# A fused attention and expert kernel: two PSUM banks become one tile, and copies at two seams are regrouped

## The chip, the cores and the metric

The kernel runs on one core of one Trainium2 chip. The metric is the device time of one execution in microseconds (us); the time given for a kernel is the median of several executions. A profiled execution shows a span, from its first to its last instruction, and a granted clock of TensorE.

## The reference

The first half is causal attention over blocks of 64 rows: 8 batches of 8 heads, 576 rows of 64 values each. The second half sends every one of the 4608 rows to one of 8 experts.

```python
scores = scale * np.matmul(q, k.transpose(0, 1, 3, 2))   # B=8 H=8 S=576 D=64
mask = block_i >= block_j                                 # blocks of 64 rows
...
attn_out = np.matmul(softmax(scores), v)
x = attn_out.transpose(0, 2, 1, 3).reshape(B * S, H * D)  # 4608 x 512
logits = x @ w_gate                                       # 8 experts
expert_idx = np.argmax(logits, axis=1)
gate_w = probs[np.arange(N), expert_idx]
...
h = np.maximum(x_sorted[lo:hi] @ w1[e], 0.0)              # 512 -> 1024
y_sorted[lo:hi] = h @ w2[e]                               # 1024 -> 512
return gate_w[:, None] * y
```

## The kernel before

**Attention** goes by pairs of heads, 32 of them. A loop over p holds the steps of one pair and of its neighbours, and the order in which the loop is written is the order of each engine's queue (the schedule is manual; only the semaphore waits are put in by the framework, which finds them from which tiles instructions read and write). In step p TensorE (PE) computes scores(p+1), which ScalarE (ACT) turns into exponentials; then attend(p), ten or so products with V, first into `o0` (128 columns of the PSUM bank `mix`) and then into `oP` (another bank); then trans(p+2), nine transposes of the next Q and K into the bank `sA`, which `copies` moves to SBUF; then turn_back(p-1), logits(p-1) and denominators(p). GpSimd (POOL) casts Q and K of pair p+2 to 16 bits in `h16`, of which there is one buffer. `keep(p)` copies `o0` and `oP` to SBUF on ACT in two instructions (L307 and L308). `s4` is two strips of 64 score columns, one at the end of `mix` and one at the end of `oP`, with one exponential each.

Once per batch, in six pairs of the loop and again near its end, the step also holds shares() (an exponential on ACT, L391), ranks() (matmuls into columns 192 to 239 of `mix`, L402 and L406) and count(). They choose the experts of the batch before. These pairs are called ranked pairs below; in a ranked pair ranks() stands in PE's queue right behind trans(p+2).

**The opening** does pairs 0 and 1 ahead of the loop. The transposes of pair 1 go to `oP` (eight) and `mix` (one), and VectorE (DVE) copies the two parts to SBUF. Then POOL makes the constants of attention and of routing, and `wg`, and only then comes the loop, whose first step holds the cast of pair 2 (L222 on POOL).

**The hand-over** is the last step of the loop and what follows. Rows sorted by expert are worked on in pages of 128: m1 (L634) multiplies with w1, m2 (L645) with w2. The stationary operand of m1 is first copied out of the weight store `wall` by mstage (128x4096 in 16 bits), for page 0 on ACT (L626) and for page 1 and all later ones on DVE (L627). mexpert loads the page's expert number into a register. Page 0's m1 is cut in two halves around the last turn_back and logits; settle (L338) reads the strip that logits and denominators write in the bank `sB`, and m1(1) writes over that bank.

Of the kernel before, what the change touches and what calls it, by code (L numbers as in the profile page):

```python
# [15 lines left out]
ds = bass.ds  # L16
# [6 lines left out]
def kernel(  # L23
# [40 lines left out]
    sC = psum.tile([128, 2, 512], F32, name="sC")  # L64
    oP = psum.tile([128, 512], F32, name="oP")
    mix = psum.tile([128, 512], F32, name="mix")
    sA16, sB16, sC16 = (t.rearrange("p h f -> p (h f)").bitcast(F16) for t in (sA, sB, sC))
    back = sC.rearrange("p h f -> p (h f)")
    o0, s4, strip = mix[:, 0:128], (mix[:, 128:192], oP[:, 448:512]), sB[:, 0, 0:160]

# [191 lines left out]
    def scores(p):  # L262

        pt, acc, p4, qkT = pts[p % 2], accs[p % 2], p4s[p % 2], qkTs[p % 2]
        a, b, c = ((t[:, 0], t[:, 1]) for t in (sA, sB, sC))
        low = slice(0, 64)
        for h in range(2):
            r = slice(h * 64, h * 64 + 64)
            nc.tensor.matmul(out=s4[h], lhsT=qkT[r, 1, 448:576], rhs=qkT[r, 0, 512:576],
                             start=True, stop=True, skip_group_check=True)  # L270
        for h in range(2):
            exp(p4[:, h], s4[h])
        score(p, 0, a, 0, 128, 448)
        score(p, 0, a, 448, 0, 64)
        exp(pt[:, :, 0:448], sA[:, :, 0:448])
        exp(acc[low, :, 0:64], sA[low, :, 448:512])
        score(p, 2, c, 256, 320, 256)
        score(p, 0, c, 0, 64, 64)
        score(p, 1, c, 64, 128, 64)
        score(p, 3, c, 128, 384, 64)  # L280
        score(p, 2, c, 192, 256, 64)
        exp(pt[:, :, 1152:1408], sC[:, :, 256:512])
        exp(low_blocks(pt[low]), sC[low, :, 64:192].rearrange("p h (c x) -> p h c x", c=2))
        exp(pt[low, :, 1088:1152], sC[low, :, 192:256])
        exp(acc[:, :, 64:128], sC[:, :, 0:64])
        score(p, 1, b, 0, 192, 384)
        score(p, 3, b, 384, 448, 128)
        exp(pt[:, :, 512:896], sB[:, :, 0:384])
        exp(pt[:, :, 960:1088], sB[:, :, 384:512])
# [14 lines left out]

    def keep(p):
        oT = oTs[p % 2]
        nc.scalar.activation(oT[:, 0:128], o0, AF.Copy)  # L307
        nc.scalar.activation(oT[:, 128:576], oP[:, 0:448], AF.Copy)  # L308

# [274 lines left out]
    tags = [t[:, 256:258] for t in xss]  # L584
    stages = [t.rearrange("p h f -> p (h f)").bitcast(F16)[:, 0:4096] for t in pts]
    hTs = [t.rearrange("p n f -> p (n f)")[:, 0:1024] for t in qkTs]
    ys = [t.rearrange("p c h d -> p (c h d)")[:, 0:512] for t in vts[0:3]] + \
# [35 lines left out]

    def mstage(T, engine=nc.vector):
        src = wall[:, ds(pg["e", T], 1), 0:8, :].rearrange("p a n f -> p (a n f)")
        did = nc.scalar.activation(stages[T % 2], src, AF.Copy) if engine is nc.scalar \  # L626
            else engine.tensor_copy(stages[T % 2], src)  # L627
        read_of(did, T)

    def m1(T, part=range(8)):  # L630
        hp = hps[T % 2]
        for f in part:
            for c in range(4):
                nc.tensor.matmul(  # L634
                    out=hp[:, f // 4, f % 4 * 128:f % 4 * 128 + 128],
                    lhsT=stages[T % 2][:, c * 1024 + f * 128:c * 1024 + f * 128 + 128],
                    rhs=xTs[T % XS][:, c, :], start=(c == 0), stop=(c == 3),
                    skip_group_check=True)
# [42 lines left out]
    with tc.manual_schedule(engines={ET.PE, ET.Activation, ET.DVE, ET.Pool, ET.SP}):  # L681
# [11 lines left out]
        trans(0, ((sC16, 0, 5), (sB16, 5, 9)), (nc.scalar, nc.vector))()  # L693
        cast(1, (nc.vector, 0, 5), (nc.gpsimd, 5, 9))
        scores(0)
        trans(1, ((oP.bitcast(F16), 0, 8), (mix.bitcast(F16), 8, 9)), (nc.vector, nc.vector))()
        for _ in range(12):
            nc.tensor.transpose(sA16[:, 0:128], ident16, ident16)
        constants()
        routing_constants()  # L700
        for h in range(2):
            r = slice(h * 64, h * 64 + 64)
            nc.sync.dma_start(
                out=gate[r], in_=moe_w_gate.rearrange("(p h d) e -> h d p e", h=2, d=64)[h])
            nc.gpsimd.tensor_copy(wg[r, :, h * E:h * E + E], gate[r, :, ::-1])
        slots_of = [p for p in range(3, PAIRS - 5) if p % HP < 3]
# [10 lines left out]
        for p in range(PAIRS + 1):  # L717
# [17 lines left out]
            if p + 2 < PAIRS:  # L735
                cast(p + 2)
            for b, j in scatters.get(p, ()):
                scatter(b, j)
# [9 lines left out]
            if left == 1:  # L748
                mexpert(0, ET.Activation)
                mstage(0, nc.scalar)  # L750
            if nxt:
# [3 lines left out]
            if now:  # L755
                attend(p)
                keep(p)
                sums(p)
            if p == PAIRS:
                m1(0, range(0, 4))  # L760
            if left == 3:
                weigh()
            turned = trans(p + 2) if p + 2 < PAIRS else None
            if done >= 0 and ranked:
# [29 lines left out]
            if left == 3:  # L794
                first_rows()
            if left == 1:
                mexpert(1)
                mstage(1)
        rest = rest_pages()
# [58 lines left out]
```

## Time and profile before

| What | Value |
|---|---|
| time, median of 3 | 354.7 us (354.23 to 354.81) |
| the profiled execution | 354.11 us |
| its span, and what lies around it | 352.2 us, 1.9 us |
| granted clock, mean | 0.993 |
| PE busy | 331.8 us, 94% of the span |
| ACT busy | 239.0 us, 68% |
| DVE busy | 225.1 us, 64% |
| POOL busy | 172.6 us, 49% |

The shares are means over three parts that have different limits: the opening (to about 20 us), the pairs (20 to 200 us) and the pages (from about 208 us). In the rows further down a row of the timeline gives the start of a group of like instructions, its length, the engine, the line, what is written and read, the count, and in brackets the idle time of the engine just before it with what ended it. Ends of matmuls are modelled.

### The profile page before, as it was taken

What the parts mean: (1) busy time and instruction counts of PE and PEld (TensorE: products, weight loads), DVE (VectorE), ACT (ScalarE), POOL (GpSimd) and SP (SyncE); (2) the same over time, 40 slices, a digit from 0 to 9 for tenths busy, and PEclk for the clock granted to TensorE, in tenths of its full rate; (3) what the DMA queues carried; (4) which work ended last, traced back from release to release, by engine and by line L of the source; (5) the groups of instructions that cost most, each with busy time, mean ns of one, the idle gap of its engine ahead of it and who ended that gap; (6) DMA issues with size and microseconds to landing.
All of it is one profiled execution on the core that took longest, in us unless ns stands there. A gap on an engine that the chain in (4) does not pass through costs nothing. (4 is left out here: it accounts for less than half of the span.)

```text
span 352.2 us, 11512 instructions
## 1 busy us (share of the span) xinstructions
PE 331.8 (94%) x4232; PEld 226.0 (64%) x4232; DVE 225.1 (64%) x516; ACT 239.0 (68%) x533; POOL 172.6 (49%) x216
## 2 busy tenths in 40 slices
PE   5899999999999999999999989899999999999980
PEld 4566666676666576656666567567677777777750
DVE  3557688788787887887889988683343434433330
ACT  3889898989898989989888824343454545544540
POOL 2821426647547557475586058768434342233231
PEclk9999999999999999999999999999999999999997
DMA  8999999999999999999999959999999899343531
GB/s 174 216 216 215 211 218 224 251 247 260 255 241 232 248 231 242 238 253 246 240 194 215 133 84 171 181 210 155 182 199 178 162 144 182 77 138 96 111 87 52
DMA packets 96803, 67.04 MB, mean 190 GB/s; under 512 B 71776, under 2 KB 80992, under 8 KB 96736
## 3 DMA queue, kind: packets, MB, share of 16 engines
q1 hardware_dynamic: 78816, 34.62, 52.5%
q0 software_dynamic: 17632, 30.98, 44.3%
q8 instruction: 37, 0.61, 0.8%
q10 hardware_dynamic: 288, 0.59, 0.7%
q14 instruction: 30, 0.25, 0.3%
HBM read 61.93 MB, written 15.77 MB: 221 GB/s over the span
## 5 line engine op out<-in xcount | busy, mean ns | idle before, releaser
L627 DVE COPY pt<-wall 128x4096 f16 x39 | 50.0, 1283 | 69.8 <-PE sB L634 33.4
L634 PEld LDWEIGHTS <-pt 128*128 128x128 f16 x1216 | 70.8, 98 | 12.2 <-issue 2.5
L300 PE MATMUL oP<-pt,v 128*64 128x448 f32 (+2 forms) x320 | 50.8, 459 | 0.0
L645 PEld LDWEIGHTS <-qkT 128*128 128x128 f16 x304 | 28.2, 98 | 28.3 <-ACT qkT L640 1.0
L640 ACT ACTIVATE qkT<-sA 128x1024 f16<-128x1024 f32 x19 | 19.4, 1023 | 36.5 <-PE sA L634 28.1
L427 POOL DMA_INDIRECT xsorted<-x,slot x30 | 37.3, 1243 | 11.4 <-POOL slot L426 7.9
L222 POOL CAST h<-qk 128x1152 f16<-128x1152 f32 (+2 forms) x20 | 22.3, 1114 | 38.8 <-PE sA L235 19.1
L634 PE MATMUL sB<-qk,pt 128*128 128x128 f16 x608 | 37.6, 219 | 2.4 <-DVE lr L338 1.3
L640 ACT ACTIVATE qkT<-sB 128x1024 f16<-128x1024 f32 x19 | 19.4, 1022 | 29.0 <-PE sB L634 29.0
L300 PEld LDWEIGHTS oP<-pt,v 128*64 128x64 f32 x320 | 22.5, 137 | 23.4 <-issue 18.4
L221 ACT ACTIVATE qkT<-sA 128x576 f16<-128x576 f16 x60 | 35.8, 650 | 2.3 <-PE sA L235 0.9
L634 PE MATMUL sA<-qk,pt 128*128 128x128 f16 x608 | 37.2, 219 | 0.0
L645 PE MATMUL sC<-wall,qkT 128*128 x152 | 35.9, 379 | 0.6 <-ACT qkT L640 0.6
L645 PE MATMUL oP<-wall,qkT 128*128 x152 | 35.9, 379 | 0.3 <-issue 0.2
L260 ACT ACTIVATE pt<-sB 128x768 f32<-128x768 f32 x64 | 35.0, 614 | 0.0
L654 POOL DMA_INDIRECT out_dram<-v,to x18 | 19.7, 1094 | 27.9 <-ACT v L650 26.0
L260 ACT ACTIVATE pt<-sC 128x512 f32<-128x512 f32 (+2 forms) x96 | 32.6, 414 | 0.9 <-PE mix L300 0.7
L300 PE MATMUL oP<-pt,wall 128*64 128x448 f32 (+2 forms) x192 | 30.4, 459 | 0.0
L260 ACT ACTIVATE pt<-sA 128x896 f32<-128x896 f32 x32 | 29.4, 918 | 0.2
L358 DVE TENSOR_TENSOR x<-sC,rec 128x640 f16<-128x640 f32 x24 | 19.8, 824 | 15.2 <-PE sC L352 14.5
L222 POOL CAST h<-wall 128x1152 f16<-128x1152 f32 x12 | 13.7, 1142 | 26.3 <-PE sA L235 16.8
L426 POOL TENSOR_SCALAR slot<-sl 128x1 int32<-128x1 f32 x40 | 14.4, 359 | 19.7 <-DVE sm L395 19.5
(185 smaller groups left out, 608.9 us busy)
## 6 DMA issues: line engine op xcount, KB each, us to landing
wall<-in_moe_w_dram POOLq DMA_DIRECT2D x32, 512.0 KB
qk<-in_q_dram SPq DMA_DIRECT2D x20, 288.0 KB
v<-in_v_dram SPq DMA_DIRECT2D x44, 128.0 KB
qk<-in_k_dram SPq DMA_DIRECT2D x18, 288.0 KB
wall<-in_v_dram SPq DMA_DIRECT2D x28, 128.0 KB
wall<-in_q_dram SPq DMA_DIRECT2D x12, 288.0 KB
wall<-in_k_dram SPq DMA_DIRECT2D x12, 288.0 KB
xsorted<-v SPq DMA_DIRECT2D x2, 516.0 KB
```

What stands on the lines that cost most here:

```text
L221: return nc.scalar.activation(dst, src, AF.Copy)
L222: return engine.tensor_copy(dst, src)
L260: nc.scalar.activation(dst, src, AF.Exp, scale=scale)
L300: nc.tensor.matmul(out=o[h * 64:h * 64 + 64], lhsT=vt[:, c, h, :] if c < 4 else v4[:, 2 * (p % HP) + h, :], rhs=src[:, h], start=(c == 0), ...
L358: nc.vector.tensor_tensor(out=x16[:, :, hp * 128:hp * 128 + 128].rearrange("p i (h d) -> p i h d", h=2), in0=back[:, 0:640].rearrange("p ( ...
L426: nc.gpsimd.tensor_single_scalar(slot, small[f"sl{b % 2}"][:, j:j + 1], 128.0, op=ALU.add)
L427: did = nc.gpsimd.indirect_dma_start(out=xsorted[:, :], out_offset=bass.IndirectOffsetOnAxis(ap=slot[0:m, :], axis=0), in_=x16s[b % 3][0:m ...
L627: else engine.tensor_copy(stages[T % 2], src)
L634: nc.tensor.matmul(out=hp[:, f // 4, f % 4 * 128:f % 4 * 128 + 128], lhsT=stages[T % 2][:, c * 1024 + f * 128:c * 1024 + f * 128 + 128], r ...
L640: nc.scalar.activation(hTs[T % 2], hp.rearrange("p a f -> p (a f)"), AF.Relu)
L645: did = nc.tensor.matmul(out=yp, lhsT=hT[:, f * 128:f * 128 + 128], rhs=wall[:, ds(pg["e", T], 1), 8 + f, :].rearrange("p a f -> p (a f)") ...
L654: did = nc.gpsimd.indirect_dma_start(out=out[:, :], out_offset=bass.IndirectOffsetOnAxis(ap=to, axis=0), in_=y, in_offset=None, bounds_che ...
```

## The change

Four edits.

1. The banks `mix` and `oP` become the two halves of one tile `out2`, and the two strips of `s4` are read by one exponential. `keep` is split into keep_first and keep_rest, with the same two copies.
2. In the opening the transposes of pair 1 lie in one piece in `out2`, and DVE copies them in two instructions of 576 columns (K, then Q). The cast of pair 1 is divided seven to two between DVE and POOL, it was five to four. The routing constants and `wg` stand behind the cast of pair 2 (the third cast).
3. In the step p = 0 the copies of trans(2) go to two engines, K to DVE and Q to ACT. Both had been on ACT.
4. At the hand-over ACT copies the w1 of page 0 in two halves, the second between keep_first and keep_rest, and then that of page 1 in three pieces into three buffers that are free by then; DVE no longer copies page 1.

```diff
-    oP = psum.tile([128, 512], F32, name="oP")
-    mix = psum.tile([128, 512], F32, name="mix")
-    sA16, sB16, sC16 = (t.rearrange("p h f -> p (h f)").bitcast(F16) for t in (sA, sB, sC))
+    out2 = psum.tile([128, 2, 512], F32, name="out2")
+    mix, oP = out2[:, 0], out2[:, 1]
+    sA16, sB16, sC16, out16 = (t.rearrange("p h f -> p (h f)").bitcast(F16)
+                               for t in (sA, sB, sC, out2))
     back = sC.rearrange("p h f -> p (h f)")
-    o0, s4, strip = mix[:, 0:128], (mix[:, 128:192], oP[:, 448:512]), sB[:, 0, 0:160]
+    o0, s4, strip = mix[:, 0:128], out2[:, :, 448:512], sB[:, 0, 0:160]
...
-        for h in range(2):
-            exp(p4[:, h], s4[h])
+        exp(p4, s4)
...
-    def keep(p):
-        oT = oTs[p % 2]
-        nc.scalar.activation(oT[:, 0:128], o0, AF.Copy)
-        nc.scalar.activation(oT[:, 128:576], oP[:, 0:448], AF.Copy)
+    def keep_first(p):
+        nc.scalar.activation(oTs[p % 2][:, 0:128], o0, AF.Copy)
+
+    def keep_rest(p):
+        nc.scalar.activation(oTs[p % 2][:, 128:576], oP[:, 0:448], AF.Copy)
...
+    stage_apart = [accs[0].rearrange("p h q -> p (h q)").bitcast(F16),
+                   qkTs[1].rearrange("p n f -> p (n f)"), h16.rearrange("p c f -> p (c f)")]
...
+    def mstage_half(T, half):
+        read_of(nc.scalar.activation(stages[T % 2][:, 2048 * half:2048 * half + 2048],
+                                     w1_of(T, 4 * half, 4 * half + 4), AF.Copy), T)
+
+    def mstage_apart(T):
+        for to, a, b in ((stage_apart[0], 0, 4), (stage_apart[1], 4, 6), (stage_apart[2], 6, 8)):
+            read_of(nc.scalar.activation(to[:, 0:(b - a) * 512], w1_of(T, a, b), AF.Copy), T)
+
+    def stationary(T, c):
+        if T == 1:
+            return stage_apart[max(c - 1, 0)][:, (c == 1) * 1024:(c == 1) * 1024 + 1024]
+        return stages[T % 2][:, c * 1024:c * 1024 + 1024]
...
-                    lhsT=stages[T % 2][:, c * 1024 + f * 128:c * 1024 + f * 128 + 128],
+                    lhsT=stationary(T, c)[:, f * 128:f * 128 + 128],
...
-        cast(1, (nc.vector, 0, 5), (nc.gpsimd, 5, 9))
+        cast(1, (nc.vector, 0, 7), (nc.gpsimd, 7, 9))
         scores(0)
-        trans(1, ((oP.bitcast(F16), 0, 8), (mix.bitcast(F16), 8, 9)), (nc.vector, nc.vector))()
+        trans(1, ((out16, 0, 9),), (nc.vector, nc.vector))()
...
         constants()
-        routing_constants()
...
-            nc.gpsimd.tensor_copy(wg[r, :, h * E:h * E + E], gate[r, :, ::-1])
...
             if p + 2 < PAIRS:
                 cast(p + 2)
+            if p == 0:
+                routing_constants()
+                for h in range(2):
+                    r = slice(h * 64, h * 64 + 64)
+                    nc.gpsimd.tensor_copy(wg[r, :, h * E:h * E + E], gate[r, :, ::-1])
...
             if left == 1:
                 mexpert(0, ET.Activation)
-                mstage(0, nc.scalar)
+                mstage_half(0, 0)
...
             if now:
                 attend(p)
-                keep(p)
+                keep_first(p)
+                if left == 1:
+                    mstage_half(0, 1)
+                keep_rest(p)
+                if left == 1:
+                    mexpert(1, ET.Activation)
+                    mstage_apart(1)
                 sums(p)
...
-            turned = trans(p + 2) if p + 2 < PAIRS else None
+            turned = trans(p + 2, engines=(nc.scalar, nc.scalar if p else nc.vector)) \
+                if p + 2 < PAIRS else None
...
-            if left == 1:
-                mexpert(1)
-                mstage(1)
```

The order below is that of the built programs. Names in it are tiles, with a number of the buffer behind; "waits" lists on which engines' semaphores an instruction waits. The line numbers of the changed file are higher, by one at the top and more further down.

**ScalarE in a ranked pair.** These are the last exponential of the pair, shares, the two copies of keep and the two copies of trans, before:

```order
L260 ACTIVATE pt_77<-sB 128x2x384 [waits DVE_49,PE_49]
L260 ACTIVATE pt_77<-sB 128x2x128 [waits Activation_49]
L391 ACTIVATE ex<-d 128x40 [waits DVE_49]
L307 ACTIVATE oT_83<-mix 128x128 [waits PE_49,Activation_49]
L308 ACTIVATE oT_83<-oP 128x448 [waits PE_49,Activation_49]
L221 ACTIVATE qkT_74<-sA 128x576 [waits PE_49,Activation_49]
```

and of the change:

```order
L261 ACTIVATE pt_76<-sB 128x2x384 [waits DVE_49,PE_49]
L261 ACTIVATE pt_76<-sB 128x2x128 [waits Activation_49]
L392 ACTIVATE ex<-d 128x40 [waits DVE_49]
L306 ACTIVATE oT_82<-out_67 128x128 [waits PE_49,Activation_49]
L309 ACTIVATE oT_82<-out_67 128x448 [waits Activation_49]
L222 ACTIVATE qkT_73<-sA 128x576 [waits PE_49,Activation_49]
```

The order is the same, but both copies now read one tile, and of the two only the first waits for PE. Its wait counts the last product of attend, where before it counted the products into `o0`, and L308 counted the last.

**TensorE in the same pair**, at the end of trans and the start of ranks, before:

```order
L235 MATMUL sA<-ident_94,h_73 128x128
L402 LDWEIGHTS before_95 [waits DVE_49]
L402 MATMUL mix<-oh_89,before_95 128x40 [waits Activation_49]
L406 LDWEIGHTS ones_96
L406 MATMUL mix<-oh_89,ones_96 128x40
```

and of the change:

```order
L236 MATMUL sA<-ident_93,h_72 128x128
L403 LDWEIGHTS before_94 [waits DVE_49]
L403 MATMUL out_67<-oh_88,before_94 128x40 [waits Activation_49]
L407 LDWEIGHTS ones_95
L407 MATMUL out_67<-oh_88,ones_95 128x40
```

The rows stand where they stood. The matmul's wait for ACT counted to L307 before, and counts to keep_rest (L309) now, since that too reads the tile which ranks writes.

**ScalarE at the hand-over**, from keep_rest of pair 30 to page 0's ReLU, before:

```order
L308 ACTIVATE oT_83<-oP 128x448
L621 TENSOR_LOAD first_e
L626 ISA
L626 ACTIVATE pt_76<-wall 128x4096
L391 ACTIVATE ex<-d 128x40
L307 ACTIVATE oT_84<-mix 128x128
L308 ACTIVATE oT_84<-oP 128x448
L640 ACTIVATE qkT_74<-sA 128x1024
```

and of the change, from the first half of page 0's w1 on:

```order
L634 ACTIVATE pt_75<-wall 128x2048
L392 ACTIVATE ex<-d 128x40
L306 ACTIVATE oT_83<-out_67 128x128
L634 ISA
L634 ACTIVATE pt_75<-wall 128x2048
L309 ACTIVATE oT_83<-out_67 128x448
L624 TENSOR_LOAD first_e
L639 ISA
L639 ACTIVATE acc<-wall 128x2048
L639 ISA
L639 ACTIVATE qkT_74<-wall 128x1024
```

The second half stands between the two copies of keep, and behind them a register load and three pieces of page 1 (the third, into `h_72`, and the ReLU follow). 

**GpSimd in the opening**, before:

```order
L132 MEMSET wall 64x512
masks.py:65 MEMSET before_95 128x128
masks.py:66 AFFINE_SELECT before_95<-before_95 128x128
L136 MEMSET ones_96 128x128
...
L150 COPY base<-region 128x8
L705 COPY wg<-gate 64x4x8 x2
L222 CAST h_73<-qk_2_72 128x2x9x64
```

and of the change:

```order
L133 MEMSET wall 64x512
L223 CAST h_72<-qk_2_71 128x2x9x64
masks.py:65 MEMSET before_94 128x128
masks.py:66 AFFINE_SELECT before_94<-before_94 128x128
L137 MEMSET ones_95 128x128
...
L151 COPY base<-region 128x8
L755 COPY wg<-gate 64x4x8 x2
```

The cast of pair 2 stood behind seventeen small instructions and the two copies of `wg`; it stands ahead of them now.

## Rows read from the trace of the kernel before

**Rows 1.** Busy time by stretch: PE, PEld, DVE, ACT, POOL; clock, DMA, GB/s

```profile
20.00:200.00 180.00, 178.98 (x2493) 115.22 (x2487) 146.71 (x345) 160.75 (x424) 95.88 (x111) 1.00 1.15 232
```

**Rows 2.** Timeline of the opening, pairs 1 and 2

```profile
7.65 0.72 DVE L222 COPY qkT<-sB 128x512 f16<-128x512 f16 x1 [1.24 <-PE sB L235]
...
8.54 0.64 PE L255 MATMUL sA<-qkT 64*128 64x448 f16 x4
...
11.10 1.23 DVE L222 COPY qkT<-oP 128x1024 f16<-128x1024 f16 x1 [1.95 <-PE mix L235]
...
12.24 0.71 DVE L222 COPY qkT<-mix 128x128 f16<-128x128 f16 x1
...
13.01 0.20 PE L269 MATMUL mix<-qkT 64*128 64x64 f16 x1 [0.62 <-DVE qkT L222]
...
13.05 0.38 PE L255 MATMUL sA<-qkT 64*128 64x448 f16 x4
...
16.23 1.14 POOL L222 CAST h<-qk 128x1152 f16<-128x1152 f32 x1
...
16.44 0.28 PE L300 MATMUL oP<-wall,v 128*64 128x64 f32 x4
...
17.43 0.68 PE L235 MATMUL sA<-ident,h 128*128 128x128 f16 x9 [0.71 <-POOL h L222]
...
18.21 1.19 ACT L221 ACTIVATE qkT<-sA 128x576 f16<-128x576 f16 x2 [0.89 <-PE sA L235]
...
19.45 0.19 PE L269 MATMUL mix<-qkT 64*128 64x64 f16 x1 [0.66 <-ACT qkT L221]
```

**Rows 3.** Timeline of an ordinary pair: second copy of keep, copies of trans

```profile
29.17 0.55 ACT L308 ACTIVATE oT<-oP 128x448 f32<-128x448 f32 x1 [0.15 <-PE oP L300]
...
29.77 1.19 ACT L221 ACTIVATE qkT<-sA 128x576 f16<-128x576 f16 x2
```

**Rows 4.** Timeline of the first ranked pair: keep, trans, ranks, copies of trans

```profile
52.44 0.29 ACT L307 ACTIVATE oT<-mix 128x128 f32<-128x128 f32 x1
...
52.60 0.68 PE L235 MATMUL sA<-ident,h 128*128 128x128 f16 x9
52.77 0.55 ACT L308 ACTIVATE oT<-oP 128x448 f32<-128x448 f32 x1
...
53.11 0.18 PE L402 MATMUL mix<-oh,before 128*128 128x40 f16 x1
...
53.37 1.19 ACT L221 ACTIVATE qkT<-sA 128x576 f16<-128x576 f16 x2
```

**Rows 5.** Timeline of the hand-over: pair 31, pages 0 and 1

```profile
197.54 3.62 ACT L626 ACTIVATE pt<-wall 128x4096 f16 x1 [0.66 <-DMA wall<-in_moe_w_dram]
...
200.57 0.31 PE L300 MATMUL oP<-wall 128*64 128x64 f32 x4
...
201.19 0.26 ACT L307 ACTIVATE oT<-mix 128x128 f32<-128x128 f32 x1
201.34 0.53 ACT L308 ACTIVATE oT<-oP 128x448 f32<-128x448 f32 x1
201.50 0.18 PE L402 MATMUL mix<-oh,before 128*128 128x40 f16 x1 [0.61 <-DVE wall L314]
...
205.24 1.07 PE L634 MATMUL sA<-qk,pt 128*128 128x128 f16 x16
...
206.40 1.02 ACT L640 ACTIVATE qkT<-sA 128x1024 f16<-128x1024 f32 x1 [4.52 <-PE sA L634]
...
207.11 0.34 DVE L338 STREAM_TRANSPOSE lr<-sB 128x160 f32<-128x160 f32 x1
...
207.58 1.61 PE L634 MATMUL sB<-qk,pt 128*128 128x128 f16 x26 [1.28 <-DVE lr L338]
```

**Rows 6.** Busy time by stretch, as rows 1: hand-over, and the end

```profile
200.00:210.00 10.00, 8.11 (x127) 6.65 (x124) 8.28 (x22) 3.29 (x6) 4.11 (x6) 1.00 0.68 74
...
347.00:353.00 6.00, 0.00 (x0) 0.00 (x0) 0.00 (x0) 0.00 (x0) 0.00 (x0) 0.54 0.03 9
```

More of the change, by code (lines that the diff above doesn't have):

```diff
@@ L268, in scores @@
             r = slice(h * 64, h * 64 + 64)
-            nc.tensor.matmul(out=s4[h], lhsT=qkT[r, 1, 448:576], rhs=qkT[r, 0, 512:576],
+            nc.tensor.matmul(out=s4[:, h], lhsT=qkT[r, 1, 448:576], rhs=qkT[r, 0, 512:576],
                              start=True, stop=True, skip_group_check=True)
-        for h in range(2):
-            exp(p4[:, h], s4[h])
+        exp(p4, s4)
         score(p, 0, a, 0, 128, 448)
@@ L622, in mexpert, with w1_of, mstage @@
                                     max_val=E - 1, skip_runtime_bounds_check_because=why)
[L624 to L628, printed above, removed]
+    def w1_of(T, a, b):
+        return wall[:, ds(pg["e", T], 1), a:b, :].rearrange("p a n f -> p (a n f)")
+    def mstage(T):
+        read_of(nc.vector.tensor_copy(stages[T % 2], w1_of(T, 0, 8)), T)
+    def mstage_half(T, half):
[8 more added lines that the diff above has]
+        return stages[T % 2][:, c * 1024:c * 1024 + 1024]
     def m1(T, part=range(8)):
@@ L699 @@
         constants()
-        routing_constants()
         for h in range(2):
-            r = slice(h * 64, h * 64 + 64)
             nc.sync.dma_start(
-                out=gate[r], in_=moe_w_gate.rearrange("(p h d) e -> h d p e", h=2, d=64)[h])
-            nc.gpsimd.tensor_copy(wg[r, :, h * E:h * E + E], gate[r, :, ::-1])
+                out=gate[64 * h:64 * h + 64],
+                in_=moe_w_gate.rearrange("(p h d) e -> h d p e", h=2, d=64)[h])
         slots_of = [p for p in range(3, PAIRS - 5) if p % HP < 3]
```

## The prediction

> **What bounds the kernel now.** I read the busy time by stretch first. From 20 to 200 us PE is busy for 178.98 of 180 us, and ACT, the next, for 160.75 [rows 1]. A microsecond in which PE stands still there is added to the time almost whole, and one saved on ACT or DVE is worth nothing unless PE waited for it. So the question for each edit is: where does PE wait now, and where will it? For that I read the timeline at four places: the opening, an ordinary pair, a ranked pair, the hand-over. In rows 2 the reader is to see two brackets on PE, 0.62 us for pair 1's copies and 0.71 us for the cast of pair 2, and one of 0.66 us for pair 2's copies; in rows 4, that PE goes from trans to ranks with no bracket at all; in rows 5, brackets of 0.61 and 1.28 us. Times below are worked out against the profiled execution (354.11 us). The median of the runs is 0.6 us above it, and I add that at the end.
>
> **One tile instead of two banks, in an ordinary pair.** The first copy of keep now waits for the last product of attend, as the order of ACT shows. L308, which waits for that product now, starts at 29.17 [rows 3]. After the change keep_first starts there, and keep_rest right behind: at the hand-over, where neither of the two has anything to wait for, they start 0.15 apart (201.19 and 201.34) [rows 5]. keep_rest thus runs from about 29.33 for 0.55 us, and like them it lets the next instruction start some 0.13 before its end, at 29.75. The copies of trans start at 29.77 now, because trans itself ends then. They are not late, and PE sees nothing: cost 0. If that cover of 0.02 us failed, a few hundredths in 26 pairs would be at stake.
>
> The single exponential for the two strips saves one ACT instruction a pair. ACT has about 19 us to spare in rows 1, and PE computes the rest of the scores while the strips are read. I put it at nothing; the most it could give is what ACT could pass on to PE, whose idle time in some 30 pairs is 1.0 us altogether [rows 1].
>
> **One tile, in the six ranked pairs.** Here ranks stands behind trans on PE, and its first matmul writes the tile that keep_rest still reads. Before, it waited for the first copy alone, done at 52.44 + 0.29 = 52.73, long before ranks started at 53.11: no wait [rows 4]. Afterwards keep_first starts at 52.77 (where L308, which waited for the same product, starts now), keep_rest at 52.92, and it ends at 52.92 + 0.55 = 53.47. With 0.06 us for the signal (as in rows 2, below) ranks starts at 53.53, and PE has nothing else in its queue. That is 53.53 - 53.11 = 0.42 us a pair, **+2.5** for six (the other five look like this one). From below: trans, which the row ends at 52.60 + 0.68 = 53.28, may really have held PE until then, and the loss is 0.25 a pair, 1.5. From above: with a signal of 0.15, as in the bracket of rows 3, 0.5 a pair, 3.0. I take 2.5, since starts are recorded and ends of matmuls are modelled. The copies of trans start at 53.37 now and could start at 52.92 + 0.42 = 53.34: they add nothing.
>
> A rule of the Trainium skill bears on this wait. The page PSUM — Partial Sum Buffer, section "PSUM bank collisions raise a hardware error", says to guard PSUM by bank and quadrant of partitions, not by address. The trace agrees as far as it goes: L307 reads `mix` from 52.44 on, 0.33 before the last product into `oP` lets L308 go. By that rule ranks, which writes the bank of `mix`, need not wait for keep_rest, which reads the other, and the 2.5 would be nothing; by the built waits, which go by the tile, it is 2.5.
>
> **The opening.** Pair 1: DVE copies 1024 and then 128 columns from 11.10, and scores(1) starts at 13.01, 1.91 later; the second copy begins 0.09 before the first one's end (12.24, 12.33), and 0.06 pass from its end (12.95) to scores(1) [rows 2]. Two copies of 576 take their place. Rows 2 have 0.72 us for 512 columns and 1.23 for 1024, so 0.72 + 64/512 x 0.51 = 0.78 for 576. Two of them with the same overlap, and 0.06 for the signal, give 1.53: scores(1) at 12.63, **-0.38**. Attend(0), which ends at 16.72 now, ends at about 16.35.
>
> Pair 2: its cast runs on POOL from 16.23 to 17.37, and trans(2) waits for it until 17.43. Ahead of the constants it can start as soon as trans(1) has read `h16`, by 11.2, and be done by 12.4. Then trans(2) follows attend(0) at once: the 0.71 of the bracket goes, **-0.71**. The constants and `wg` are then done 1.15 us later than now, about 17.4, where only the cast of pair 3 is behind them, for which `h16` comes free at about the same time. From trans(2)'s start to scores(2) it is 19.45 - 17.43 = 2.02 now. Afterwards K is copied by DVE (0.78) and Q by ACT (0.6, half of the 1.19). They look parallel, but both write one tile, and in the built program ACT's copy waits for DVE's. So: 0.78 until the first copy starts (18.21 - 17.43), 0.78, signal 0.06, 0.65, signal 0.06, together 2.33, **+0.33**. The opening sums to -0.38 - 0.71 + 0.33 = **-0.75**. Bounds: were a DVE copy of 576 as quick as ACT's 0.6, then -0.65 - 0.71 + 0.1 = -1.3; were it as dear as the 1024 columns (1.23), +0.6. I stay by the 512 row, which is nearest.
>
> **The hand-over.** ACT's copy of page 0's w1 is 4096 columns in 3.62 us; 1024 columns take 1.02 (the ReLU) [rows 5], so a half is about 1.02 + 1024 x 2.60/3072 = 1.89. The first half runs from 197.54 to 199.4, and ACT is free before attend(31) ends, at 200.88. But keep_first cannot start before 201.0, a tenth after that. The second half stands behind it, from about 201.15 to 203.0; keep_rest stands behind that and ends at 203.45; and ranks waits for keep_rest. It starts at 203.5, not 201.50: **+2.0** at this place, where PE stands still for 2.6 us. All PE work to the end of m1(0) hangs on it: 205.24 + 1.07 = 206.31 becomes 208.3. What is given back: m1(1) waits until 207.58 now, 1.28 us, because DVE copies page 1's w1 and only then runs settle (207.11), which frees the bank. Afterwards DVE is free for settle as soon as logits is done. That stands ahead of the half of m1(0) that starts at 205.24, so with 2.0 more it is done by 207.3, and settle by 207.7. ACT's pieces: 203.45, 0.66 for register and addresses as in the bracket of rows 5, then 1.89 + 1.02 + 1.02, done at 208.0. Both are in time for m1(1) at 208.35. Net 208.35 - 207.58 = **+0.8**. It is 0.6 if a half is half of 3.62 and signals are short, and 1.3 if the register load holds the pieces up by another half microsecond. From there on pages follow on PE, and nothing gives the 0.8 back.
>
> **Sum.** -0.75 + 2.5 + 0.8 = +2.55: 356.66 by the profiled execution, and with 0.6, **357.2** against the median.
>
> **The rivals.**
>
> *Waits by bank* (the other side). If ranks is released by keep_first alone, the ranked pairs cost nothing. At the hand-over keep_first runs at 201.0 at the latest, ranks loses at most 0 and saves up to 0.6 of the 0.61, and m1(1) starts when the last piece is there: half 2 and keep_rest end near 202.3 if keep_first is let go by the products into `o0`, plus 0.66 + 3.93 = 206.9, 0.7 before 207.58. Then -0.75 - 0.7 = -1.45, and 353.3 against the median. For it: the two banks are separate memories, and L307 reads one while PE fills the other. Against it: the second copy has lost its wait for PE in the built order, which only makes sense if the first waits for all. It decides if ranks starts before keep_rest's end.
>
> *The 0.42 is absorbed.* If the products behind ranks had been waiting for something else anyway, six stalls vanish: -0.75 + 0.8 = 0.05, and 354.8. For it: some PE idle time exists in that stretch. Against it: only 1.0 us in 30 pairs.
>
> *The clock falls.* After the last matmul the granted clock is 0.54 over the last 6 us, and in the opening four products of 448 columns take 0.64 us where they later take 0.38, the lower level (1.2 GHz) [rows 2, 6]. Between 200 and 210, with 0.61 and 1.28 us of standing still, it stays at 1.00 [rows 6], the 2.4 GHz level. The 2.6 us in one piece lies between these cases. If it fell and the next 3 us of PE work ran 0.64/0.38 times as long, that is +2.0: 359.2. The Trainium skill, TensorE: Matmul & The Clock Gate, section "Why this matters for your kernels", advises against idle gaps of PE between bursts of matmuls; the trace agrees for the end of the kernel and does not show it for gaps as short as rows 5 have.
>
> *The early cast does not come early.* If pair 2's Q and K are not there by 11.2, or DVE and POOL hold each other up, trans(2) stays where it is and only the +0.33 is left: +3.6, and 358.3.
>
> **How the numbers follow.** Forecast 0.68; waits by bank 0.08; absorbed 0.11; clock 0.05; no early cast 0.08. The range is 354.8 to 358.6: below, it takes in the absorbed case and the sum with each term at its low end (-1.3 + 1.5 + 0.6, 355.5); above, the late cast and the sum with the opening at its dear end (+0.6 + 2.5 + 0.8, 358.6). Outside are waits by bank and the clock, 0.13. A measurement here can tell some 0.2% from no change, 0.7 us. Waits by bank is the faster case, 0.08; absorbed is the case of no change, 0.11; the rest, 0.81, is slower.
>
> **What would show it.** Right: in ranked pairs a bracket on ranks of some 0.3 to 0.4 us that names ACT and keep_rest; at the hand-over ranks near 203.5 less what the opening and ranked pairs shift, behind the second half and keep_rest; in the opening trans(2) with no bracket and scores(2) some 0.75 earlier. Wrong: ranks with no bracket, or DVE's copies of 576 columns at 1.0 or more.

## The result

| | Before | Changed |
|---|---|---|
| time, median (range, runs) | 354.75 us (354.23 to 355.57, 4) | 358.81 us (355.67 to 360.73, 4) |
| ratio, 95% interval | | 1.0109 (1.006 to 1.0159) |
| profiled execution, span | 354.11 us, 352.2 us | 358.3 us, 356.5 us |
| mean granted clock | 0.993 | 0.981 |

The change makes the kernel slower by about 1.1%. The direction was forecast, but 358.81 lies 0.2 us above the range that was given (354.8 to 358.6), and 1.6 us above the value. Executions more than 1.5% above the fastest of their kernel are left out of every ratio and interval here, which weighs most on e5 (7 of 12 left out; its median over all twelve is 353.01 us, and 350.17 for the kernel before) and on e3 (6 of 13), and the profiles of e3 and e11 are of such executions.

**The ranked pair**, in the timeline of the changed kernel (answers to [rows 4]):

```profile
51.14 0.68 PE L236 MATMUL sA<-ident,h 128*128 128x128 f16 x9
51.31 0.28 ACT L306 ACTIVATE oT<-out 128x128 f32<-128x128 f32 x1 [0.20 <-PE out L300]
51.49 0.54 ACT L309 ACTIVATE oT<-out 128x448 f32<-128x448 f32 x1
...
51.91 1.20 ACT L222 ACTIVATE qkT<-sA 128x576 f16<-128x576 f16 x2
52.08 0.18 PE L403 MATMUL out<-oh,before 128*128 128x40 f16 x1 [0.26 <-ACT oT L309]
```

ranks (L403) has a bracket now that names keep_rest. It starts 0.94 us after trans does; before, it was 53.11 - 52.60 = 0.51. That is the 0.42 of the prediction, to a hundredth. From the first product of scores(p) to that of scores(p+1), a ranked pair takes 6.50 us where it took 6.08 (6.02 in pair 15). Of the six, pairs 15 and 23 take still more, 6.88 and 6.78.

**The opening** (answers to [rows 2]):

```profile
10.41 1.42 DVE L223 COPY qkT<-out 128x576 f16<-128x576 f16 x2 [1.31 <-ACT pt L261]
...
11.88 0.24 PE L270 MATMUL out<-qkT 64*128 64x64 f16 x2 [0.30 <-DVE qkT L223]
...
12.29 1.55 POOL L223 CAST h<-qk 128x1152 f16<-128x1152 f32 x1 [1.42 <-DMA qk<-in_k_dram]
...
15.61 0.68 PE L236 MATMUL sA<-ident,h 128*128 128x128 f16 x9
...
16.40 0.76 DVE L223 COPY qkT<-sA 128x576 f16<-128x576 f16 x1 [0.89 <-PE sA L236]
...
17.19 0.65 ACT L222 ACTIVATE qkT<-sA 128x576 f16<-128x576 f16 x1 [0.75 <-DVE qkT L223]
...
17.89 0.21 PE L270 MATMUL out<-qkT 64*128 64x64 f16 x2 [0.92 <-ACT qkT L222]
```

DVE copies 576 columns in 0.76 us (forecast 0.78). trans(2) at 15.61 has no bracket, and ACT's copy of Q waits for DVE's copy of K: 2.28 us from trans(2) to scores(2), forecast 2.33. The cast of pair 2 waits until 12.29 for K to land, which was not foreseen and costs nothing here. scores(2) starts 1.56 us earlier than before, twice the forecast, but scores(0) starts 0.47 earlier in this execution too (at 8.04; before, at 8.51, just ahead of the 8.54 of [rows 2]), ahead of anything that the change does to PE. Counted from scores(0), scores(2) comes 9.85 us later, and came 10.94 later before.

**The hand-over** (answers to [rows 5]; the second fence is busy time by stretch, PE, PEld, DVE, ACT, POOL, clock, DMA, GB/s):

```profile
202.40 0.31 PE L300 MATMUL out<-wall 128*64 128x64 f32 x4
...
202.81 0.28 ACT L306 ACTIVATE oT<-out 128x128 f32<-128x128 f32 x1 [1.39 <-PE out L300]
...
202.99 1.90 ACT L634 ACTIVATE pt<-wall 128x2048 f16 x1
...
204.78 0.54 ACT L309 ACTIVATE oT<-out 128x448 f32<-128x448 f32 x1
205.21 1.91 ACT L639 ACTIVATE acc<-wall 128x2048 f16 x1
205.37 0.18 PE L403 MATMUL out<-oh,before 128*128 128x40 f16 x1 [2.66 <-ACT oT L309]
...
207.58 1.89 PE L650 MATMUL sA<-qk,pt 128*128 128x128 f16 x16
...
210.71 1.07 PE L650 MATMUL sA<-qk,pt 128*128 128x128 f16 x16
...
211.61 0.28 PE L650 MATMUL sB<-qk,acc 128*128 128x128 f16 x2
```

```profile
204.00:206.00 2.00, 0.63 (x11) 0.62 (x10) 0.42 (x2) 2.00 (x3) 0.00 (x0) 1.00 0.54 62
206.00:208.00 2.00, 2.00 (x32) 1.27 (x31) 1.30 (x3) 2.00 (x3) 0.00 (x0) 0.66 0.09 9
208.00:210.00 2.00, 2.00 (x18) 2.00 (x17) 0.99 (x8) 1.01 (x2) 0.23 (x2) 0.50 0.34 63
210.00:212.00 2.00, 2.00 (x34) 1.57 (x33) 1.12 (x3) 0.19 (x1) 1.70 (x3) 0.98 0.50 122
...
232.00:234.00 2.00, 2.00 (x6) 0.66 (x5) 1.86 (x6) 0.46 (x1) 2.00 (x3) 0.51 0.32 93
```

The copies stand as forecast: half of w1, keep_rest behind it, ranks behind that, PE still for 2.66 us (forecast 2.6). What was held unlikely follows: the granted clock falls from 1.00 to 0.50, which is 1.2 GHz, soon after PE starts again, and the first half of m1(0) takes 1.89 us where the second takes 1.07. m1(1) starts at 211.61, 4.03 later than before. In the pages the clock falls once more, at 231 to 234 us, behind three gaps of about 0.5 us on PE for which the profile shows no releaser and one of 0.49 for a ReLU. The kernel before has three such gaps, of 0.3 to 0.4 us, at 223 to 225, and no fall. In the last part of the span 1.7 us come back: from the last product (342.48 and 348.47) to the end of the span it is 9.7 us before and 8.0 after.

### The profile page after: what moved, and what is told of

Its sections match the earlier page's. It is cut to its first block, busy times and chain, and to the rows that moved or that the text cites. A ratio compares the mean times of both kernels' runs of the same rounds, so it can differ in the third digit from the quotient of the medians.

```text
span 356.5 us, 11432 instructions
## 1 busy us (share of the span) xinstructions
PE 334.5 (94%) x4232; PEld 227.2 (64%) x4232; DVE 226.2 (63%) x516; ACT 238.2 (67%) x504; POOL 171.3 (48%) x216
## 4 chain that ended last, share of the span: by engine, by line
PE 78%; SPq 4%; DVE 2%; ACT 2%; another core or an unknown queue 2%; DMA 1%; issue 1%; POOL 0%; ACTq 0%; DVEq 0%
PE out L300 21%; PE out L661 9%; PE sC L661 9%; PE sA L650 9%; PE sB L650 9%; PE sB L326 7%; PE sC L353 4%; PE sA L236 3%; PE sB L256 2%; SPq L605 2%; PE sA L256 2%; PE sC L256 2%; DMA qk<-xsorted 1%; PE out L270 1%
## 5 line engine op out<-in xcount | busy, mean ns | idle before, releaser
L631 DVE COPY pt<-wall 128x4096 f16 x38 | 48.5, 1278 | 71.4 <-PE sB L650 34.4
L650 PEld LDWEIGHTS <-pt 128*128 128x128 f16 x1184 | 69.7, 98 | 12.1 <-issue 2.9
L300 PE MATMUL out<-pt,v 128*64 128x448 f32 (+2 forms) x320 | 50.8, 459 | 0.0
L656 ACT ACTIVATE qkT<-sA 128x1024 f16<-128x1024 f32 x19 | 19.4, 1023 | 35.1 <-PE sA L650 23.6
L223 POOL CAST h<-qk 128x1152 f16<-128x1152 f32 (+1 forms) x20 | 22.6, 1131 | 40.7 <-PE sA L236 22.7
L650 PE MATMUL sA<-qk,pt 128*128 128x128 f16 x608 | 38.1, 221 | 0.5 <-DMA qk<-xsorted 0.5
L661 PE MATMUL out<-wall,qkT 128*128 x152 | 37.3, 390 | 0.5 <-ACT qkT L656 0.5
L300 PEld LDWEIGHTS out<-pt,v 128*64 128x64 f32 x320 | 22.5, 137 | 23.4 <-issue 18.5
L650 PE MATMUL sB<-qk,pt 128*128 128x128 f16 x576 | 35.7, 219 | 1.5 <-issue 1.5
L656 ACT ACTIVATE qkT<-sB 128x1024 f16<-128x1024 f32 x19 | 19.4, 1023 | 26.5 <-PE sB L650 26.5
L300 PE MATMUL out<-pt,wall 128*64 128x448 f32 (+2 forms) x192 | 30.4, 459 | 0.0
L427 POOL TENSOR_SCALAR slot<-sl 128x1 int32<-128x1 f32 x40 | 13.4, 335 | 22.1 <-DVE sm L396 21.8
```

Source lines behind the costliest of these rows:

```text
L223: return engine.tensor_copy(dst, src)
L300: nc.tensor.matmul(out=o[h * 64:h * 64 + 64], lhsT=vt[:, c, h, :] if c < 4 else v4[:, 2 * (p % HP) + h, :], rhs=src[:, h], start=(c == 0), ...
L631: read_of(nc.vector.tensor_copy(stages[T % 2], w1_of(T, 0, 8)), T)
L650: nc.tensor.matmul(out=hp[:, f // 4, f % 4 * 128:f % 4 * 128 + 128], lhsT=stationary(T, c)[:, f * 128:f * 128 + 128], rhs=xTs[T % XS][:, c ...
L656: nc.scalar.activation(hTs[T % 2], hp.rearrange("p a f -> p (a f)"), AF.Relu)
L661: did = nc.tensor.matmul(out=yp, lhsT=hT[:, f * 128:f * 128 + 128], rhs=wall[:, ds(pg["e", T], 1), 8 + f, :].rearrange("p a f -> p (a f)") ...
```

## Experiments

Chips differ here: the kernel before takes about 355 us in the result and on the chip of e7 to e10, and 350 us on three others (that of e1 to e4, that of e5, e6 and e13 to e15, that of e11 and e12). Which chip the result was taken on is not on record. So each kernel is compared by its ratio to the kernel before on its own chip.

**e4, one tile alone.** The kernel before with edit 1:

```diff
-    oP = psum.tile([128, 512], F32, name="oP")
-    mix = psum.tile([128, 512], F32, name="mix")
+    out2 = psum.tile([128, 2, 512], F32, name="out2")
+    mix, oP = out2[:, 0], out2[:, 1]
...
-        for h in range(2):
-            exp(p4[:, h], s4[h])
+        exp(p4, s4)
```

> The kernel before with edit 1 alone (one tile for the two banks, one exponential for the strips; pair 1's transposes still eight and one). Theory: six ranked pairs at 6.50 instead of 6.08, +2.5, and 0.4 more at the hand-over, where ranks waits for the second copy of keep; no fall of the clock: 357.2 to 357.8. Rival (waits by bank, or the wait is hidden): 354.5 to 355.

Measured: 1.0079 (1.0036 to 1.0123), 352.83 against 350.3 us. All six ranked pairs take 6.50 us, and the rows of one read as in the changed kernel:

```profile
52.65 0.54 ACT L308 ACTIVATE oT<-out 128x448 f32<-128x448 f32 x1
...
53.24 0.18 PE L402 MATMUL out<-oh,before 128*128 128x40 f16 x1 [0.26 <-ACT oT L308]
```

The one tile alone costs its 2.5 us in the ranked pairs and 0.4 at the hand-over (15.60 us from scores(31) to m1(1), before 15.20); by the interval the loss is 1.3 to 4.3 us. Waits by bank and an absorbed 0.42 are both out.

**e2 and e9, ranks elsewhere in PE's queue.** The changed kernel with ranks behind logits (e2) or between turn_back and logits (e9):

```diff
-            if done >= 0 and ranked:
-                ranks(done)
-                count()
             if old:
                 turn_back(p - 1)
...
             if old:
                 logits(p - 1, not now)
+            if done >= 0 and ranked:
+                ranks(done)
+                count()
```

> The changed kernel with ranks and count moved behind turn_back and logits in the ranked pairs and at the hand-over. Theory: ranks waits for the second copy of keep only because nothing stands between trans and ranks; 1.2 us of other work put between them hides 0.42 us in each of six pairs (period of a ranked pair 6.50 to about 6.1), so -2.5, and takes 1.2 of the 2.66 us at the hand-over away, so that the clock stays at 1.00 there: together -4 to -5.5, 353.3 to 354.8. Rival: the ranked pairs are long for another reason, and only the hand-over gains: 356 to 357.

> The changed kernel with ranks between turn_back and logits (count behind finish). Theory: turn_back (0.72 us, same shape of the array as ranks) covers the 0.42 us, and the change of shape that cost 0.3 where ranks stood behind logits is not there: ranked pairs at 6.05 to 6.15 instead of 6.50, and the standing still at the hand-over 2.0 instead of 2.7, shared out over two places. 0.0 to 0.4% slower than before. Rival: a ranked pair stays at 6.4 or more, so that the place in the queue is not what matters.

Measured: e2 1.0035 (0.9997 to 1.0073), e9 1.0193 (1.014 to 1.0246). Both expectations fail for the ranked pairs: they take 6.40 us in both (6.51 in pair 15), and so not 6.1. The rows of e2 show where it went:

```profile
54.65 0.17 DVE L415 TENSOR_TENSOR base<-out,base 128x8 f32<-128x8 f32 x1
...
54.93 0.12 PEld L270 LDWEIGHTS <-qkT 64*128 64x128 f16 x2 [0.35 <-issue]
54.96 0.20 PE L270 MATMUL out<-qkT 64*128 64x64 f16 x2
```

The next product that writes the tile is that of the strips (L270). It now waits until count (L415) has read the ranks out of it: in e2 it starts 0.14 after L415's end, though the bracket names no releaser, and in e9 the bracket there is 0.30 and names L415. Moved back, ranks no longer waits, but its reader is late, and the wait passes to the next user of the same tile. I had put the rest of e2's loss down to a change of the array's shape when e9 went out; that was wrong, since in e9 ranks stands behind turn_back and the wait is there all the same. e2's ratio is nevertheless below those of the changed kernel (1.0083 to 1.0146, on other chips): 1.1 us of its standing still at the hand-over is filled (a bracket of 1.55), the clock stays at 1.00 behind it, and pairs 15 and 23 have lost their extra time. In e9, pairs 9, 13, 17, 21 and 25 are also 0.3 to 0.6 us longer than 5.90; in pair 9 DVE starts settle 0.77 us late and PE waits for it. Why there, I did not find. At the hand-over of e9 PE stands still for 1.96 us ahead of ranks, and behind it the granted clock falls, as it does in the changed kernel:

```profile
208.00:210.00 2.00, 2.00 (x25) 1.51 (x18) 1.04 (x6) 2.00 (x3) 0.00 (x0) 0.50 0.20 31
```

The clock falls once more in its pages, from 231 to 235 us. Together these account for a part of e9's 1.0193; how large a part was not worked out.

**e5, the hand-over alone, and e3, all but the one tile.** e5 is the kernel before with edit 4; e3 the changed kernel with edit 1 undone (the diff of e4 turned round, and pair 1's transposes in eight and one again).

> The kernel before with edit 4 alone: ScalarE copies the first page's w1 in halves and the second page's in three pieces; two tiles, opening as before. Theory: the halves do no harm where ranks waits for the first copy of keep alone; TensorE's 0.61 and 1.28 us there shrink by 0.5 to 1.2 together: 353.5 to 354.3. Rival: the pieces on ScalarE or what they bring forward cost by themselves: 355.5 or more.

> The changed kernel with edit 1 undone (two tiles, two exponentials for the strips, pair 1's transposes in eight and one as before); opening order and hand-over as in the change. Theory: ranks waits for the first copy of keep alone, so the ranked pairs are back at 6.08, the hand-over has no stall of over 1.3 us and no fall of the clock; only the opening's gain is left (scores of pair 2 earlier by 0.5 to 1.2) and some of the hand-over's 1.28: 352.5 to 353.8, faster than both. Rival: the hand-over's copies on ScalarE themselves cost the time: 356 or more.

Measured: e5 0.9962 (0.9932 to 0.9993), e3 0.9964 (0.9911 to 1.0017). By the ratio e5 is a little faster than the kernel before; e3's interval takes in no change. In e5:

```profile
198.91 0.26 ACT L306 ACTIVATE oT<-mix 128x128 f32<-128x128 f32 x1
199.07 1.90 ACT L634 ACTIVATE pt<-wall 128x2048 f16 x1
...
200.00 0.31 PE L300 MATMUL oP<-wall 128*64 128x64 f32 x4
200.24 0.19 PE L403 MATMUL mix<-oh,before 128*128 128x40 f16 x1
...
200.87 0.53 ACT L309 ACTIVATE oT<-oP 128x448 f32<-128x448 f32 x1
...
205.45 0.28 PE L650 MATMUL sB<-qk,acc 128*128 128x128 f16 x2
```

keep_first runs while attend goes on, the second half of w1 goes in its shadow, and ranks starts before keep_rest. From scores(31) to m1(1) it takes 13.65 us (205.45 - 191.80), before 15.20: -1.55. The same copies in the same order give 1.55 us here; on one tile they cost 0.6 (in e13 below, where the clock stays at 1.00). The 1.55 is not had in every execution. In e3's profile the ranked pairs are at 6.08 but for pair 15 (6.46) and ranks has no bracket, yet m1(0) waits 0.64 for a page's rows and m1(1) starts 15.26 us after scores(31), no earlier than before.

**e6, the second half behind keep_rest**, on the changed kernel:

```diff
-                if left == 1:
-                    mstage_half(0, 1)
                 keep_rest(p)
                 if left == 1:
+                    mstage_half(0, 1)
                     mexpert(1, ET.Activation)
```

> The changed kernel with the second half of the first page's w1 behind the second copy of keep instead of ahead of it. Theory: ranks no longer waits behind 1.9 us of copying, its wait falls from 2.66 to about 0.75 us, and the clock stays at 1.00 there; the first page then waits up to 0.5 us for its second half and the second page up to 1.5 us for its pieces, so the gain is 1 to 2.5 against the change: 356.3 to 357.8; the ranked pairs' +2.5 stay. Rival: the same copies wait in another place, as long in one piece, and nothing is gained: 358 to 359.

Measured: 1.0066 (1.0044 to 1.0088); the changed kernel is at 1.0122 on the same chip (e13), and the two intervals overlap a little. ranks' bracket is 0.86 and the clock stays at 1.00, as expected; page 0 does not wait, and page 1 waits 0.52 for its last piece. m1(1) starts 14.01 us after scores(31), 1.8 earlier than in e13, so most of the stall belongs to the place of the second half. What is left is about what e4 costs.

**e8, the opening alone** (edits 2 and 3 on the kernel before, with two tiles, so pair 1 in eight and one):

> The kernel before with edits 2 and 3 alone, but two tiles (pair 1's transposes eight and one): cast of pair 1 seven to two, constants behind the third cast, pair 2's K copied by DVE. Theory by the profiles so far: the third cast waits for K of pair 2 to land (12.3 us), trans(2) follows attend(0) without a bracket, the copies one after the other take 0.3 more; scores of pair 2 start 0.3 to 0.5 us earlier than before, pairs 15 and 23 may lose 0.3: 0.0 to -0.15%. Rival, as predicted: 0.75 us, -0.2%.

Measured: 1.0012 (0.9982 to 1.0042): no difference to be told. trans(2) starts 0.30 earlier (17.13), DVE and ACT copy one after the other, and scores(2) starts at 19.40, before 19.45. Pair 15 takes 6.46, before 6.02; settle starts 0.55 us late in it.

```profile
13.06 0.62 PE L255 MATMUL sA<-qkT 64*128 64x448 f16 x4
...
96.77 0.35 DVE L339 STREAM_TRANSPOSE lr<-sB 128x160 f32<-128x160 f32 x1 [0.55 <-ACT wall L260]
...
97.17 0.40 PE L255 MATMUL sB<-qkT 64*128 64x384 f16 x4 [0.34 <-issue]
```

The first of these rows belongs to scores(1). In [rows 2] the same four products take 0.38, and by the end of attend(0) this execution is 0.47 us behind for that reason, which hides most of what the opening gives. With the 0.4 us of pair 15 little is left of it in the time.

**e1, e12, e14 against e7, e11, e13: the clock.** The changed kernel with work in the stall, and the changed kernel unaltered:

```diff
+            if left == 1:
+                for _ in range(36):
+                    nc.tensor.transpose(sA16[:, 0:128], ident16, ident16)
             if done >= 0 and ranked:
                 ranks(done)
```

> The changed kernel with 36 transposes of the identity put into TensorE's queue ahead of ranks in pair 31 (they write a bank that is free there, and add nothing to the result). Theory: the 2.66 us in which TensorE stands still at the hand-over let the clock fall, and the fall costs about 1.5 us. The wait for the second copy of keep stays, so ranks starts at the same place, but the granted clock from 200 to 216 us is 1.00 instead of 0.89, 16 products of the first page take 1.07 us and not 1.89, and the time is about 1.5 us below the changed kernel's (357.0 to 357.5). Rival: the clock falls there for another reason, or the standing still costs only its own length; then the time stays at 358 to 359.

> The changed kernel unaltered, on one chip with the three below and with the kernel before. Theory: ranked pairs at 6.50 us and a standing still of 2.7 us at the hand-over again, and the clock falls behind it again, so that 16 products of the first page take 1.89 us and not 1.07; 1.0 to 1.2% slower than before, and 0.4 to 0.6% slower than the run with the transposes in the stall (1.0052). Rival: the fall of the clock was a chance of the one profiled execution; then 0.5 to 0.7% slower, like that run.

> The changed kernel once more, beside the kernel with transposes in its stall on one chip, since the two were timed on different chips so far. Theory: the fall of the clock behind the 2.7 us costs 1.5 us: 0.4 to 0.5% slower than its neighbour. Rival: the clock costs what the profile shows, but something else that the two chips do differently made up the 0.9% between the two ratios; then they differ by 0.4 to 0.5% here and both ratios move together. Second rival: no difference, below 0.2%.

> The changed kernel with 36 transposes of the identity in the stall at the hand-over (they add nothing to the result), on the same chip as the changed kernel. Theory: 0.4 to 0.5% faster than that, granted clock 1.00 from 205 to 212 us, and products of the first page at 1.07 us for 16. Rival: within 0.2% of it.

> The changed kernel on one chip with the two below. Theory: its fixed loss is about 2.5 us in the ranked pairs and 0.5 to 1 at the hand-over, less 0.4 at the opening, 0.8% together; where the clock falls behind the 2.7 us (two of three profiled executions so far), another 1.5 us, 1.2 to 1.4% together. On a chip where it falls, it is 0.4% or more slower than the neighbour with transposes; on one where it doesn't, within 0.2%. Rival: the clock makes no difference to the median on either kind of chip.

> The changed kernel with 36 transposes of the identity in the stall (they add nothing to the result). Theory: granted clock 1.00 between 205 and 212 us, 0.6 to 1.0% slower than before on any chip. Rival: it moves with the changed kernel, whatever the clock does.

| Kernel, chip by time of before | Ratio (95%) | Clock behind the stall | ranks to m1(1) |
|---|---|---|---|
| changed, result, 355 | 1.0109 (1.006 to 1.0159) | falls, 0.50 | 6.24 us |
| changed, e7, 355 | 1.0146 (1.0101 to 1.0191) | falls, 0.50 | 6.21 us |
| changed, e11, 350 | 1.0083 (1.0043 to 1.0122) | 1.00 | 4.65 us |
| changed, e13, 350 | 1.0122 (1.0079 to 1.0165) | 1.00 | 4.64 us |
| with transposes, e1, 350 | 1.0052 (1.001 to 1.0093) | 1.00 | 4.65 us |
| with transposes, e12, 350 | 1.0101 (1.0051 to 1.0151) | 1.00 | 4.64 us |
| with transposes, e14, 350 | 1.0083 (1.0059 to 1.0107) | 1.00 | 4.64 us |

Rows of e7 and then of e13:

```profile
205.54 0.18 PE L403 MATMUL out<-oh,before 128*128 128x40 f16 x1 [2.66 <-ACT oT L309]
...
208.50 1.45 PE L650 MATMUL sA<-qk,pt 128*128 128x128 f16 x16
```

```profile
205.53 0.18 PE L403 MATMUL out<-oh,before 128*128 128x40 f16 x1 [2.66 <-ACT oT L309]
...
207.31 1.07 PE L650 MATMUL sA<-qk,pt 128*128 128x128 f16 x16
...
210.17 0.28 PE L650 MATMUL sB<-qk,acc 128*128 128x128 f16 x2
```

The same 2.66 us of standing still let the clock fall in two of four profiled executions, both where the kernel before takes 355 us, and not in two on 350 us chips. Where it falls, the way from ranks to m1(1) is 1.6 us longer, shown twice. With transposes in the stall the clock stays at 1.00 in three of three, but all three are on 350 us chips, where it stayed without them too; on no chip with a fall was that kernel run. The expectations on the clock hold in e1, e7, e12 and e14, though the 16 products shown of e7 take 1.45 us and not 1.89, since the clock is back during them. Those of e11 to e13 on the times of neighbours are not borne out: the kernel with transposes has the higher ratio on one chip (1.0101 and 1.0083) and the lower on the other (1.0083 and 1.0122), with intervals that overlap. And the changed kernel's ratio is no lower where its profile shows no fall (1.0083 and 1.0122) than in the result (1.0109). So the price in an execution is shown; its share of the medians is not settled.

**e10 and e15, a better version.** Edits 2 and 4 on two tiles, pair 2's copies both on ACT (edits 1 and 3 undone, so pair 1 in eight and one):

> Edits 2 and 4 on two tiles, with pair 2's copies both on ScalarE as before (edits 1 and 3 undone, pair 1's transposes eight and one). Theory: hand-over -1.5 as in the run of edit 4 alone, opening -0.4 to -0.8, ranked pairs at 6.08: 0.4 to 0.7% faster than before, the best version. Rival: the opening gives nothing and only the hand-over's 0.4% is left.

> Edits 2 and 4 on two tiles, pair 2's copies both on ScalarE (edits 1 and 3 undone), on another chip than before. Theory: no wait of ranks for the second copy of keep, hand-over 1.5 us shorter than before, opening about 0.4: 0.4 to 0.8% faster than the kernel before. Rival: the 0.8% of the first chip was its own; here 0 to 0.3%.

Measured: e10 0.992 (0.9879 to 0.9961), 353.34 against 355.11 us; e15 0.9987 (0.9943 to 1.0031). Ranked pairs are at 6.08 in both. Faster than the kernel before on one chip, no difference to be told on the other, where PE waited 1.83 us for V of pair 31 and 0.80 for a page's rows at the hand-over; it is faster than the changed kernel on both (e7 and e13). From scores(31) to m1(1) it takes 14.30 us in e10, with a wait of 0.58 for a page's rows, and 16.19 in e15. So of the 1.55 us of e5's profile 0.9 is left in the one and nothing in the other.

## Why the prediction was wrong

*One tile in an ordinary pair, nothing.* Right: 5.90 us before and after.

*Six ranked pairs, +2.5.* Right: 0.42 in each of the six alone (e4) and in four of the six in the change. The waits went by the tile. The Trainium skill's rule (PSUM — Partial Sum Buffer, "PSUM bank collisions raise a hardware error") to guard by bank is what the two tiles do: in e5 PE writes the one bank at 200.24 while ACT has yet to read the other from 200.87 on.

*Pairs 15 and 23.* Not foreseen, since the sum took the other five ranked pairs to be like the first: 0.38 and 0.28 more than the others, in every run of the one tile with the new opening but e2 and e9. In pair 15 settle (L339) starts 0.55 us late on DVE, and PE waits 0.34 before the products that write its bank. This goes with edit 3: e3 and e8, which have it on two tiles, show it (6.46), and e10, e15, e4 and e5, which do not have it, show 6.08 or 6.50. In pair 23 the wait is the one of the tile: keep_first starts 0.28 later than in pair 19 behind the same last product, and the bracket of ranks is 0.54. Why DVE and ACT start late there was not found.

*The opening, -0.75.* Right on the mean. All its pieces came out (0.76 for a copy, no bracket on trans(2), 2.28 us of copies). scores(2) starts at 17.89 to 19.41 (mean 18.9) in the twelve profiles with edits 2 and 3 and at 19.15 to 19.56 (mean 19.4) in the three with the old opening, about -0.5, but scores(0), ahead of the edits, starts anywhere from 8.0 to 8.9 in them. Counted from scores(0) the means are 10.37 and 11.15 us, -0.78, with a spread of about 0.5 either way between executions. The -1.56 of the result's profile is thus half luck, and pair 15 takes 0.4 of the gain back later.

*The hand-over, +0.8.* Its working held: ranks +2.0 (in e13 11.16 us after scores(31), before 9.12), and 15.80 us to m1(1) where the clock stays, before 15.20, so +0.6. In e13 m1(1) starts at 210.17, 2.59 later than in the profile of the kernel before; the sum of the prediction was 2.55. That they agree so well is partly luck, since the two profiles are of different chips: pairs 15 and 23 cost 0.7 more in e13, and pair 29 takes 6.48 us in it where the profile of the kernel before has 6.90, as far as can be seen a difference of the chips.

*The clock, chance 0.05.* As far as the traces show, this is the step that failed: the sum put the clock at nothing. I took [rows 6], 0.61 and 1.28 us of standing still at a clock of 1.00, for evidence that 2.6 us in one piece would pass too, though I had written that it lay between the cases. In the execution whose trace is shown, and in e7, it fell, and cost 1.6 us (forecast 2.0); in e9 it fell behind 1.96 us. With it the forecast was 359.2, and 358.81 was measured. That the fall is also what put the median above the range is not shown: without a fall the changed kernel is at 1.0083 and 1.0122, and pairs 15 and 23, 0.7 us together in every profile of the unaltered change, are a second term that the sum put at nothing. My reading of the opening as the lower level rested on the length of the products alone; the granted clock in the profile is 1.00 there. The Trainium skill, TensorE: Matmul & The Clock Gate, "Why this matters for your kernels", advises against idle gaps of PE between bursts of matmuls; the trace agrees in two of the four executions of the changed kernel. The gaps that it names are longer than the 2.66 us here, so it does not settle the case.

*Behind m1(1).* The pages were taken to follow unchanged. In this execution they take 2.0 us longer, with the second fall of the clock at 231 us, and the end gives 1.7 back. e8, without the one tile and without edit 4, also has a fall there (0.62 from 226 to 230), so it is not the change's doing alone. Nor is the end: from the last product on it takes 7.9 us in e13 and 9.5 in e7, which run the same kernel. From the opening to the end the two profiles differ by -1.6 up to scores(2), +3.4 to scores(31), +2.2 to m1(1), +2.0 in the pages and -1.7 at the end, +4.3 in all (352.2 to 356.5).

## What to carry to other kernels

Where waits go by the tile, joining two buffers joins all their waits: count not only the readers that the joined instruction serves, but every later writer of either half, and expect the wait to move to the next user when an instruction is put off. A copy put between two halves of an eviction is free only as long as nothing waits for the second half; the same edit was worth up to -1.55 us on two tiles (e5) and +0.6 us on one. A stall of TensorE longer than any in the profile at hand can have a second price, the clock, that the profile does not rule out: here it fell behind 2.66 us in two of four profiles and behind 1.96 in e9, and stayed behind 1.55 in e2. Give it a real chance in the forecast, or fill the stall (that filling it keeps the clock up was not tried on a chip where it falls).

## What the hardware did unexpectedly

The same program with the same 2.66 us stall kept a granted clock of 1.00 on two chips and fell to 0.50 in the two executions where the kernel before takes 355 us. In four of the 17 profiles (the result's, e4, e5 and e7) the clock also falls to 0.50 in the opening, between 8 and 12 us. The kernel before differs by 1.4% between chips (350.15 and 355.11 us). A part of that lies in the pages: from m1(1) to the last product it is 134.8 us or more in the six profiles on the slower side and 131.6 to 132.9 in nine of the eleven on the faster side (138.0 in e11, 140.0 in e3). Pair 29 takes 6.9 us or more on the slower side and 6.5 on the faster, but for e3. And gaps of 0.3 to 0.8 us on PE, DVE and ACT that wait for nothing in the profile sit at fixed pairs of a program and move when instructions elsewhere change: pair 15 takes 6.02 us before, 6.08 with edits 2 and 4 on two tiles, and 6.46 when edit 3 is added, which alters one copy in the step p = 0.
